# Storing two weight gradients as 4 KB rows in a one-token attention and GEGLU backward kernel

## The chip, the cores and the metric

The kernel runs on one core of a Trainium2 chip. Its time is the device time of one execution in microseconds; six executions of the kernel before gave a median of 285.23 us (284.24 to 286.37). The profile is of one more execution of the same kernel, with every instruction and every DMA packet recorded. The core has a matrix engine (PE, with PEld for its weight loads), a vector engine (DVE), a scalar engine (ACT), a general engine (POOL), a queue for issuing DMAs (SyncE, SP) and 16 DMA engines.

## The reference

A layer adds two branches to its input: attention of one token over a cached window, and a GEGLU feed-forward net. The kernel returns the layer's output and the gradients of all its inputs and weights, for a given gradient `dy` of the output.

```python
xn = layernorm(x)                                  # x: 4 x 1 x 512
q  = (xn @ wq) -> 4 x 32 heads x 128               # wq: 512 x 4096
k, v = last 1024 of 4096 cached rows, 8 kv heads, each used by rep = 4 q heads
p  = softmax(q k^T / sqrt(128));  o = p v          # 4 x 32 x 128
A  = o.reshape(4, 4096) @ wo                       # wo: 4096 x 512
Bf = (gelu(xn @ w_gate) * (xn @ w_up)) @ w_down    # 512 x 1792, 512 x 1792, 1792 x 512
out = x + A + Bf
# returned: out, and d/dx, d/dk_cache, d/dv_cache, d/dwq, d/dwo, d/dw_gate, d/dw_up, d/dw_down of <out, dy>
```

Everything is bf16, sums are fp32. The gradients of the caches are 32 MB each, three quarters of them zeros (the rows outside the window). Two outputs matter here: `out_5`, the gradient of `wo`, which is `o^T dy` over the four batch rows (4096 x 512), and `out_8`, the gradient of `w_down`, which is `a^T dy` with `a` the GEGLU activation (1792 x 512). Each has rows of 512 bf16 values, 1 KB.

## The kernel before, in words

**Stages.** The kernel first loads the three feed-forward weights, does the feed-forward branch forward and backward (to line 687, some 60 us), and then loops over `t` = 0 to 3, each with two kv heads and their eight q heads. In an iteration `kv_steps` transposes the K blocks and makes the scores, `softmax` runs as a chain of small steps, `kv_steps` does the same with V for the gradient of the probabilities, `odq(t, 0)` makes `o` and `odq(t, 1)` makes `dq`, `pre(t + 1)` prepares the next iteration's `q` and `do`, and `fin` adds to the output.

**Background pieces.** The weight and cache gradients are made by small pieces of one or two matmuls, one eviction and, at the last of a group, a store. They stand in one queue, `bg`, and `tick(n)` takes the next n of them in between the foreground steps. The queue is filled with the w_down pieces (`piece_d`), the w_gate and w_up pieces (`piece_g`), and then in every iteration with those of dv, dk, wo (`piece_o`) and wq (`piece_q`). Whatever is left after the loop is run at its end.

**Row form of o and a.** `odq` leaves `o` of one kv head in a tile `od_r` whose 16 used partitions are (batch, head): for a head i of the four, only the four partitions of that head may count in `o^T dy`. Before, this is done on dy's side: `dym` holds four copies of dy, spread over the partitions and masked so that copy i is zero outside the partitions of head i (`spread_rows`, with the mask `msk_i`). `piece_o(g, i)` multiplies `od_r` with copy i into a 128 x 512 block: the 128 rows of head i. For `w_down`, `f_rows` makes the same form `a_r` from the activation: the 16 used partitions are (batch, chunk), and `piece_d(f4, i)` gives the 128 rows of chunk i of a group of four.

**Stores.** An eviction (`evac`, lines 97 and 98) goes to ACT or DVE, whichever has less planned work. The four blocks of a group lie side by side in a tile `osb`, [128, 4, 512], and are stored by one DMA on SyncE's queue. Partition p of the tile holds row p of each of the four blocks, which are 128 rows apart in the output, so the DMA writes 512 rows of 1 KB. The pool of these tiles has four buffers. Stores of zeros from one zero tile (`zero`, 1.5 MB each in rows of 12 KB, 32 in all) are put into the same queue at fixed places, and what is left of them after the loop.

**Order of work around the change.** The order on every engine is the program's. `f_rows` for the activation comes before the loops that transpose w_gate and w_up, which hold 28 slots for pieces. `spread_rows(dy4, dym)` stands between the first feed-forward matmuls and the evictions that follow. `odq(t, 0)` is followed by loads of V for t + 2 and by `pre(t + 1)`; the latter's products `domr` and `qmr` (line 324) are on POOL, and POOL also issues the loads of wo and wq for later iterations (lines 123 and 125).

Of the kernel before, what the change touches and what calls it, by code (L numbers as in the profile page):

```python
# [14 lines left out]
P = 128  # L15
# [3 lines left out]
def kernel(  # L19
# [211 lines left out]
    xnm = const.tile([P, rep, D], BF16, name="xnm")  # L231
    dym = const.tile([P, rep, D], BF16, name="dym")

    def spread_rows(src, dst):
        ps = ps_w.tile([P, D], FP32, name="row_ps", tag="w")
        nc.tensor.matmul(ps[:], lhsT=sel[:], rhs=src[:], start=True, stop=True)
        for i in range(rep):
            if i % 2:
                nc.scalar.activation(out=dst[:, i, :], in_=ps[:], func=ACT.Copy, scale=msk_i[:, i:i + 1])
            else:  # L240
                nc.vector.tensor_scalar(out=dst[:, i, :], in0=ps[:], scalar1=msk_i[:, i:i + 1], scalar2=None,
                                        op0=ALU.mult)
# [196 lines left out]
    def odq(t, k):  # L439
# [11 lines left out]
        else:  # L451
            nc.scalar.activation(out=rows[:], in_=od_ps[:, k], func=ACT.Copy, scale=scale)
        st[t][("o", "dq")[k]] = rows

    def odT(t, k):
# [30 lines left out]
    def dw(t):  # L486
        o_r, dq_r = st[t]["o"], st[t]["dq"]

        def piece_o(g, i, held):
            if i == 0:  # L490
                held["osb"] = outp.tile([P, rep, D], BF16, name="osb_o", tag="o")
            mps = ps_w.tile([P, D], FP32, name="dwo_ps", tag="w")
            nc.tensor.matmul(mps[:], lhsT=o_r[:, g, :], rhs=dym[:, i, :], start=True, stop=True)  # L493
            evac(held["osb"][:, i, :], mps[:], 512)
            if i == rep - 1:
                r0 = (t * HG + g * rep) * Dh
                store(nc.sync, out_5[r0:r0 + rep * Dh, :].rearrange("(h p) n -> p h n", p=P), held["osb"][:], "rest")

# [40 lines left out]
    for wi, wsb in enumerate((wg_sb, wu_sb)):  # L539
        for fc in range(NF):  # L540
            for c in range(ND):
                nc.tensor.matmul(hg_ps[:, wi, fc, :], lhsT=wsb[:, c, fc * P:(fc + 1) * P], rhs=xnT[:, c, :],
                                 start=(c == 0), stop=(c == ND - 1))
    spread_rows(dy4, dym)
    hgu = ffn.tile([P, 2, 4 * NF4, B], FP32, name="hgu")
# [68 lines left out]

    def f_rows(srcT, nm):

        ps = ps_w.tile([P, NF4, P], FP32, name="fr_ps", tag="w")
        for f4 in range(NF4):
            nc.tensor.matmul(ps[0:4 * B, f4, :], lhsT=srcT[:, f4].rearrange("p b i -> p (b i)"),
                             rhs=ident[:], start=True, stop=True)  # L620
        rows = const.tile([P, NF4, P], BF16, name=nm)
        nc.gpsimd.memset(rows[:], 0.0)
        evac(rows[0:4 * B], ps[0:4 * B], 512)
        return rows

    acc_sum(0, [(lambda c, fc=fc: wd_sb[:, fc, c * P:(c + 1) * P], aT_b[:, fc // 4, :, fc % 4]) for fc in range(NF)])
    a_r = f_rows(aT_b, "a_r")

    def piece_d(f4, i, n, held):
        if i == 0:  # L630
            held["osb"] = outp.tile([P, 4, D], BF16, name="osb_d", tag="o")
        mps = ps_w.tile([P, D], FP32, name="dwd_ps", tag="w")
        nc.tensor.matmul(mps[:], lhsT=a_r[:, f4, :], rhs=dym[:, i, :], start=True, stop=True)
        evac(held["osb"][:, i, :], mps[:], 512)
        if i == n - 1:
            store(nc.sync, out_8[4 * f4 * P:(4 * f4 + n) * P, :].rearrange("(h p) n -> p h n", p=P),
                  held["osb"][:, 0:n, :], "rest")
            zero(f4 == 1)
# [13 lines left out]
    for f4 in range(NF4):  # L652
        held = {}
        n = min(4, NF - 4 * f4)
        for i in range(n):
            bg.append(lambda f4=f4, i=i, n=n, held=held: piece_d(f4, i, n, held))
# [133 lines left out]
```

## Time and profile before

| What | Before |
|---|---|
| median of six executions | 285.23 us (284.24 to 286.37) |
| the profiled execution's own time, and its span | 285.14 us, 283.4 us |
| busy: PE, PEld, DVE, ACT, POOL | 202.0, 138.7, 161.1, 117.2, 29.7 us |
| DMA: bytes, packets, mean rate | 112.12 MB, 23,981, 396 GB/s |
| read from HBM, written to HBM | 30.68 MB, 81.01 MB |
| stores osb_o: count, size, median from issue to landing | 8, 512 KB, 18.7 us |
| stores osb_d | 3 of 512 KB, 1 of 256 KB, 7.5 us |
| evictions osb_o: ACT, DVE | 24 of 585 ns, 8 of 690 ns |

The busy times of engines overlap. A span runs from the first to the last instruction, and an execution's time is a little longer than it. In the profile's lines a group is named by its line in the kernel, its engine, its operation and its tiles (`out<-in`); what follows the bar is the busy time, the mean of one in ns, and the idle time in front of it with what ended it. A DMA is "issued" by a queue (SPq, POOLq, ACTq) and "lands" when all its engines have told its semaphore so. The DMA digits and shares are of 16 engines.

### The profile page before, as it was taken

What the parts mean: (1) busy time and instruction counts of PE and PEld (TensorE: products, weight loads), DVE (VectorE), ACT (ScalarE), POOL (GpSimd) and SP (SyncE); (2) the same over time, 40 slices, a digit from 0 to 9 for tenths busy, and PEclk for the clock granted to TensorE, in tenths of its full rate; (3) what the DMA queues carried; (4) which work ended last, traced back from release to release, by engine and by line L of the source; (5) the groups of instructions that cost most, each with busy time, mean ns of one, the idle gap of its engine ahead of it and who ended that gap; (6) DMA issues with size and microseconds to landing.
All of it is one profiled execution on the core that took longest, in us unless ns stands there. A gap on an engine that the chain in (4) does not pass through costs nothing.

```text
span 283.4 us, 6838 instructions
## 1 busy us (share of the span) xinstructions
PE 202.0 (71%) x2963; PEld 138.7 (49%) x2970; DVE 161.1 (57%) x310; ACT 117.2 (41%) x219; POOL 29.7 (10%) x32
## 2 busy tenths in 40 slices
PE   0455998798787889999989998999987974400000
PEld 0444676665556764567665576755556721200000
DVE  7756556476845364678566868567862774810000
ACT  2041484561144438754456645556640664400000
POOL 8400000043000420000610000500000000000000
PEclk9999599799996899999999999999995997955555
DMA  7999999999999999999999999999998999999990
GB/s 268 390 356 421 425 405 409 429 412 339 382 425 406 403 420 416 413 418 418 406 418 413 413 425 418 404 424 425 419 405 359 419 419 420 411 401 396 432 418 26
DMA packets 23981, 112.12 MB, mean 396 GB/s; under 512 B 1664, under 2 KB 10384, under 8 KB 15504
## 3 DMA queue, kind: packets, MB, share of 16 engines
q1 hardware_dynamic: 22160, 103.56, 90.2%
q0 software_dynamic: 1632, 6.29, 5.7%
q10 hardware_dynamic: 160, 1.84, 1.8%
q8 instruction: 23, 0.38, 0.5%
q14 instruction: 6, 0.05, 0.0%
HBM read 30.68 MB, written 81.01 MB: 394 GB/s over the span
## 4 chain that ended last, share of the span: by engine, by line
PE 38%; issue 19%; DMA 11%; DVE 11%; POOL 5%; ACT 3%; POOLq 0%; ACTq 0%; DVEq 0%
PE kv_ps L472 8%; DMA wq_sb<-in_A_wq_dram 7%; PE T_ps L274 7%; PE od_ps L445 5%; PE S_ps L340 5%; DMA out_dram<-stg_dv 4%; PE dwq_ps L506 2%; PE acc_ps L251 2%; DVE wqT L98 2%; PE pT_ps L274 2%; DVE dS_s L362 2%; POOL ztile L167 2%; PE dwo_ps L493 2%; PE woT_ps L274 2%; DVE T_sb L98 2%
## 5 line engine op out<-in xcount | busy, mean ns | idle before, releaser
L98 DVE COPY T_sb<-T_ps 128x1024 bf16<-128x1024 bf16 x64 | 44.1, 689 | 23.5 <-PE T_ps L274 23.4
L97 ACT CAST stg_dv<-kv_ps 128x512 bf16<-128x512 f32 x52 | 28.7, 589 | 29.1 <-PE kv_ps L472 28.4
L97 ACT CAST stg_dk<-kv_ps 128x512 bf16<-128x512 f32 x51 | 28.4, 589 | 24.4 <-PE kv_ps L472 11.0
L472 PE MATMUL kv_ps<-qmr,dS_s 128*128 128x512 bf16 x64 | 22.7, 396 | 5.9 <-ACT stg_dk L97 4.9
L324 POOL TENSOR_TENSOR domr<-r,msk 128x1024 bf16<-128x1024 bf16 x4 | 7.6, 1890 | 149.6 <-DVE r L321 120.1
L472 PE MATMUL kv_ps<-domr,P_s 128*128 128x512 bf16 x60 | 21.2, 399 | 0.2
L274 PE MATMUL T_ps<-ident,vb 128*128 128x128 bf16 x256 | 19.4, 219 | 0.3 <-DVE T_sb L98 0.3
L274 PE MATMUL T_ps<-ident,kb 128*128 128x128 bf16 x256 | 19.5, 219 | 0.2 <-issue 0.2
L274 PEld LDWEIGHTS <-kb 128*128 128x128 bf16 x256 | 16.5, 98 | 4.3 <-issue 0.9
L274 PEld LDWEIGHTS <-vb 128*128 128x128 bf16 x256 | 16.3, 98 | 4.5 <-issue 2.2
L97 ACT CAST osb_q<-dwq_ps 128x512 bf16<-128x512 f32 x26 | 15.0, 586 | 7.3 <-PE dwq_ps L506 6.1
L97 ACT CAST osb_g<-dwg_ps 128x512 bf16<-128x512 f32 (+1 forms) x26 | 12.8, 538 | 10.0 <-PE dwg_ps L645 5.0
L97 ACT CAST osb_o<-dwo_ps 128x512 bf16<-128x512 f32 x24 | 13.8, 585 | 4.3 <-PE dwo_ps L493 3.5
L98 DVE COPY wgT<-wgT_ps 128x1024 bf16<-128x1024 bf16 x14 | 9.6, 689 | 7.9 <-PE wgT_ps L274 7.8
L98 DVE COPY woT<-woT_ps 128x1024 bf16<-128x1024 bf16 x16 | 11.0, 688 | 4.3 <-PE woT_ps L274 3.9
L98 DVE CAST stg_dv<-kv_ps 128x512 bf16<-128x512 f32 x12 | 8.2, 687 | 8.6 <-PE kv_ps L472 8.4
L340 PE MATMUL S_ps<-T_sb,qm 128*32 128x256 bf16 x128 | 12.7, 386 | 0.5 <-DVE T_sb L98 0.5
L340 PE MATMUL S_ps<-T_sb,dom 128*32 128x256 bf16 x128 | 12.7, 387 | 0.0
L98 DVE CAST stg_dk<-kv_ps 128x512 bf16<-128x512 f32 x13 | 8.7, 689 | 6.8 <-DMA out_dram<-stg_dv 5.0
L472 PEld LDWEIGHTS <-dS_s 128*128 128x128 bf16 x64 | 6.1, 98 | 12.6 <-issue 11.5
L493 PE MATMUL dwo_ps<-dym,od_r 128*128 128x512 bf16 x31 | 11.8, 414 | 0.2
L98 DVE COPY wqT<-wqT_ps 128x1024 bf16<-128x1024 bf16 x16 | 10.6, 686 | 2.2 <-PE wqT_ps L274 2.1
(186 smaller groups left out, 372.6 us busy)
## 6 DMA issues: line engine op xcount, KB each, us to landing
out_dram<-ztile SPq DMA_DIRECT2D x32, 1536.0 KB, 18.9
kb<-in_A_k_cache_dram SPq DMA_DIRECT2D x8, 1024.0 KB, 13.1
vb<-in_A_v_cache_dram SPq DMA_DIRECT2D x8, 1024.0 KB, 16.8
out_dram<-stg_dv SPq DMA_DIRECT2D x8, 1024.0 KB, 16.8
out_dram<-stg_dk SPq DMA_DIRECT2D x8, 1024.0 KB, 18.5
out_dram<-osb_o SPq DMA_DIRECT2D x8, 512.0 KB, 18.7
out_dram<-osb_q SPq DMA_DIRECT2D x8, 512.0 KB, 13.3
out_dram<-osb_g SPq DMA_DIRECT2D x8, 448.0 KB, 8.4
```

Source lines behind the costliest of these rows:

```text
L97: return nc.scalar.copy(out=out, in_=in_)
L98: return nc.vector.tensor_copy(out=out, in_=in_)
L167: nc.gpsimd.memset(ztile[:], 0.0)
L251: nc.tensor.matmul(ps[:, c, :], lhsT=lf(c), rhs=rhs, start=(k == 0), stop=(k == len(terms) - 1))
L274: nc.tensor.transpose(ps[:, i, :], a, ident[:])
L324: nc.gpsimd.tensor_tensor(out=mr[:].rearrange("p g q d -> p (g q) d"), in0=r4[:, k, :].unsqueeze(1).broadcast_to([P, SL, Dh]), in1=msk[:]. ...
L340: nc.tensor.matmul(ps[b * RB:(b + 1) * RB, :], lhsT=zt[:, b * GP + g, c0:c0 + RB], rhs=T_sb[:].rearrange("p (x b) -> p b x", b=B)[:, b, :] ...
L362: nc.vector.scalar_tensor_tensor(out=out[:], in0=src[:].unsqueeze(2).broadcast_to([P, WQ, B]), scalar=rr[:, 0:1], in1=mskb[:].unsqueeze(1) ...
L445: nc.tensor.matmul(od_ps[g * 32:g * 32 + B * rep, k, g, :], lhsT=cols[:, jj, g * NQ + q, :], rhs=blks[(t, g)][:, j, :], start=(j == 0), st ...
L472: nc.tensor.matmul(mps[:].rearrange("p q d -> p (q d)"), lhsT=src[:, j * P:(j + 1) * P], rhs=mr[:, g].rearrange("p q d -> p (q d)"), start ...
L493: nc.tensor.matmul(mps[:], lhsT=o_r[:, g, :], rhs=dym[:, i, :], start=True, stop=True)
L506: nc.tensor.matmul(mps[:, i].rearrange("p g d -> p (g d)"), lhsT=xnm[:, i2 * 2 + i, c * P:(c + 1) * P], rhs=dq_r[:].rearrange("p g d -> p ...
```

## The change

The four rows that a partition of `osb` holds become four neighbouring rows of the output instead of four rows that are 128 apart. A partition then writes 4 KB in one piece.

For this, block i of a group must hold the output rows 4 p + i. The weights of its matmul are therefore every fourth column, beginning at i, of a row form that holds all four heads (or chunks) side by side, each nonzero only on its own partitions. So the mask moves from dy to `o` and `a`: `o_s` is `od_r` times the mask `msk_r` for each of the four heads, made by two products on POOL right after `od_r`; `a_s` is made from PSUM by four masked evictions of 16 rows, two on DVE and two on ACT, in place of one eviction to `a_r`. The matmul's other operand is `dyr`, dy spread over the partitions without mask, one eviction in place of the four of `dym`. The last group of w_down has two chunks of 128 rows: it becomes four blocks of 64 rows in place of two of 128, and its store has 64 partitions of 4 KB.

```diff
-    dym = const.tile([P, rep, D], BF16, name="dym")
-
-    def spread_rows(src, dst):
+    dyr = const.tile([P, D], BF16, name="dyr")
+    msk_r = const.tile([P, rep], BF16, name="msk_r")
+    nc.vector.tensor_copy(out=msk_r[:], in_=msk_i[:])
+
+    def spread_rows(src, dst, masked=True):
         ps = ps_w.tile([P, D], FP32, name="row_ps", tag="w")
         nc.tensor.matmul(ps[:], lhsT=sel[:], rhs=src[:], start=True, stop=True)
+        if not masked:
+            evac(dst[:], ps[:], 512)
+            return
         for i in range(rep):
...
         st[t][("o", "dq")[k]] = rows
+        if k == 0:
+            o_s = attw.tile([P, GP, rep, Dh], BF16, name="o_s", tag="o_s", bufs=2)
+            for g in range(GP):
+                nc.gpsimd.tensor_tensor(out=o_s[:, g], in0=rows[:, g].unsqueeze(1).broadcast_to([P, rep, Dh]),
+                                        in1=msk_r[:].unsqueeze(2).broadcast_to([P, rep, Dh]), op=ALU.mult)
+            st[t]["os"] = o_s
...
             mps = ps_w.tile([P, D], FP32, name="dwo_ps", tag="w")
-            nc.tensor.matmul(mps[:], lhsT=o_r[:, g, :], rhs=dym[:, i, :], start=True, stop=True)
+            nc.tensor.matmul(mps[:], lhsT=o_s[:, g].rearrange("p r d -> p (r d)")[:, i:rep * Dh:rep], rhs=dyr[:],
+                             start=True, stop=True)
             evac(held["osb"][:, i, :], mps[:], 512)
             if i == rep - 1:
                 r0 = (t * HG + g * rep) * Dh
-                store(nc.sync, out_5[r0:r0 + rep * Dh, :].rearrange("(h p) n -> p h n", p=P), held["osb"][:], "rest")
+                store(nc.sync, out_5[r0:r0 + rep * Dh, :].rearrange("(p i) n -> p (i n)", i=rep),
+                      held["osb"][:].rearrange("p i n -> p (i n)"), "rest")
...
-    spread_rows(dy4, dym)
+    spread_rows(dy4, dyr, masked=False)
...
-    def f_rows(srcT, nm):
+    def f_rows(srcT, nm, spread=False):
...
+        if spread:
+            rows = ffn.tile([P, NF4, 4, P], BF16, name=nm)
+            nc.gpsimd.memset(rows[:], 0.0)
+            for i in range(4):
+                if i % 2:
+                    nc.scalar.activation(out=rows[0:4 * B, :, i, :], in_=ps[0:4 * B], func=ACT.Copy,
+                                         scale=msk_i[0:4 * B, i:i + 1])
+                else:
+                    nc.vector.tensor_scalar(out=rows[0:4 * B, :, i, :], in0=ps[0:4 * B],
+                                            scalar1=msk_i[0:4 * B, i:i + 1], scalar2=None, op0=ALU.mult)
+            return rows
...
-    a_r = f_rows(aT_b, "a_r")
+    a_s = f_rows(aT_b, "a_s", spread=True)
...
+        m = n * P // 4
         mps = ps_w.tile([P, D], FP32, name="dwd_ps", tag="w")
-        nc.tensor.matmul(mps[:], lhsT=a_r[:, f4, :], rhs=dym[:, i, :], start=True, stop=True)
-        evac(held["osb"][:, i, :], mps[:], 512)
-        if i == n - 1:
-            store(nc.sync, out_8[4 * f4 * P:(4 * f4 + n) * P, :].rearrange("(h p) n -> p h n", p=P),
-                  held["osb"][:, 0:n, :], "rest")
+        nc.tensor.matmul(mps[0:m], lhsT=a_s[:, f4].rearrange("p i f -> p (i f)")[:, i:n * P:4], rhs=dyr[:],
+                         start=True, stop=True)
+        evac(held["osb"][0:m, i, :], mps[0:m], 512)
+        if i == 3:
+            store(nc.sync, out_8[4 * f4 * P:(4 * f4 + n) * P, :].rearrange("(p i) n -> p (i n)", i=4),
+                  held["osb"][0:m].rearrange("p i n -> p (i n)"), "rest")
             zero(f4 == 1)
...
-        for i in range(n):
+        for i in range(4):
             bg.append(lambda f4=f4, i=i, n=n, held=held: piece_d(f4, i, n, held))
```

More of the change, by code (lines that the diff above doesn't have):

```diff
@@ L486, in dw @@
     def dw(t):
-        o_r, dq_r = st[t]["o"], st[t]["dq"]
+        o_s, dq_r = st[t]["os"], st[t]["dq"]
         def piece_o(g, i, held):
```

## The prediction

> **What bounds the kernel now.** I read the occupancy of the page first, because no compute engine fills the span (PE 71%), and then the DMA lines under it.
>
> ```profile
> span 283.4 us, 6838 instructions
> ...
> DMA  7999999999999999999999999999998999999990
> GB/s 268 390 356 421 425 405 409 429 412 339 382 425 406 403 420 416 413 418 418 406 418 413 413 425 418 404 424 425 419 405 359 419 419 420 411 401 396 432 418 26
> DMA packets 23981, 112.12 MB, mean 396 GB/s; under 512 B 1664, under 2 KB 10384, under 8 KB 15504
> q1 hardware_dynamic: 22160, 103.56, 90.2%
> q0 software_dynamic: 1632, 6.29, 5.7%
> ```
>
> The reader is to see a DMA digit of 9 in nearly every slice, and queue shares that add up to 98% with the two small queues. The last compute instruction ends at 249.24 us (dx_b, by the timeline); from there to 283.4 only stores drain. So a microsecond of DMA work is worth up to a microsecond of the end, and compute is worth nothing until it starves the DMA engines. Next I asked for stretches, to see what each row length costs and who ends last (columns: stretch, length, busy PE, PEld, DVE, ACT, POOL, PE clock, DMA share, GB/s).
>
> ```profile
> 12.00:18.00 6.00, 3.06 (x94) 2.53 (x91) 3.31 (x10) 1.30 (x2) 0.00 (x0) 1.00 1.10 354
> 24.00:30.00 6.00, 2.52 (x64) 1.94 (x61) 4.27 (x13) 1.37 (x2) 0.00 (x0) 0.93 1.01 416
> 52.00:58.00 6.00, 5.61 (x91) 4.70 (x92) 3.03 (x6) 2.98 (x7) 0.00 (x0) 0.72 1.02 425
> ...
> 212.00:216.00 4.00, 1.91 (x24) 1.65 (x26) 2.26 (x5) 0.00 (x0) 0.00 (x0) 0.68 0.82 320
> ...
> 264.00:274.00 10.00, 0.00 (x0) 0.00 (x0) 0.00 (x0) 0.00 (x0) 0.00 (x0) 0.50 1.01 426
> 274.00:276.00 2.00, 0.00 (x0) 0.00 (x0) 0.00 (x0) 0.00 (x0) 0.00 (x0) 0.50 1.00 424
> 276.00:278.00 2.00, 0.00 (x0) 0.00 (x0) 0.00 (x0) 0.00 (x0) 0.00 (x0) 0.50 0.26 111
> 278.00:282.40 4.40, 0.00 (x0) 0.00 (x0) 0.00 (x0) 0.00 (x0) 0.00 (x0) 0.50 0.05 22
> ```
>
> 12 to 18 us moves 1 KB rows of weights (354 GB/s), 24 to 30 us 8 KB rows of K and V (416), 52 to 58 us 3.5 KB rows of osb_g among 12 KB rows of zeros (425), 264 to 274 us zeros alone (426). The last two rows matter most: a share of 0.05 is less than one of 16 engines. **One DMA engine ends last**: of the last zero store's semaphore steps in the trace, fourteen come at 276.8 to 276.9 us, one at 278.4, one at 282.4. That engine is late from 23 us on (2.5 us behind the median) and 7 us behind from 180 to 250 us, so what it has to move sets the end; a hole in the other engines' work costs nothing, unless it is longer than that lead.
>
> ```profile
> SPq L785 <- DMA out_dram<-ztile: 19.3, 5, 4.8
> ```
>
> This wait of SyncE shows the same: after the last issue it sits through five zero stores, which land 3.6 to 3.7 us apart.
>
> **The change part by part.** The sum is made against the profiled execution, 285.14 us (span 283.4 and 1.7 around it), 0.1 below the median 285.23.
>
> *Rows.* osb_o (8 x 512 KB) and osb_d (3 x 512, 1 x 256 KB) go from 5,888 rows of 1 KB to 1,472 of 4 KB; bytes, issues and their order stay. On the engine that ends last, the step from the previous store's landing to an osb_o's is 1.14 to 1.55 us, mean 1.34; to an osb_d's 1.29, 1.35, 1.38, and 0.68 for the half one (4.70 together). Rows on both sides of 4 KB: an osb_g takes 1.10 us for 448 KB (1.26 per 512 KB), a K or V load 2.49 us per MB in 8 KB rows (1.24 per 512 KB). I take 1.25 for 512 KB in 4 KB rows: 8 x 0.09 + (4.70 - 3.5 x 1.25 = 0.33) = **1.05, say 1.1 us less**. Bounds: no gain, if the steps' scatter of 0.4 us hides that stores don't pay for short rows; at most the price of 1 KB weight rows, 6.03 MB at 354 instead of 425 GB/s, 17.0 - 14.2 = 2.8 us. In between lie the packets' own durations, by size in the trace: 46 ns for 1 KB, 159 for 4 KB (q0), so 4 x 46 - 159 = 25 ns for 92 rows per engine, 2.3 us; but shares of 1.10 with 1 KB packets say that these durations overlap, so I take the landing steps.
>
> The Trainium skill, "DMA: Bandwidth & Descriptors", section Specifications, says that 512 B are enough for line rate; by it 1 KB rows lose nothing, the change gives 0 and the time stays at 285.2. The 354 GB/s above speak against it. The same page's section "Why small descriptors are slow" has some 3 cycles of overhead per packet of 32-byte beats: an estimate from it is 4 x 35 = 140 cycles against 131 per 4 KB, 6.4% of 14.2 us, 0.9 us.
>
> *a_s instead of a_r.* One 16-row eviction (0.57 us) becomes four, alternating DVE and ACT on one tile. The removed dym shows that such a set runs one after the other:
>
> ```profile
> 15.10 0.75 DVE L241 TENSOR_SCALAR dym<-row_ps,msk_i 128x512 bf16<-128x512 f32 x1 [1.73 <-PE row_ps L236]
> 16.60 0.75 DVE L241 TENSOR_SCALAR dym<-row_ps,msk_i 128x512 bf16<-128x512 f32 x1 [0.76 <-ACT dym L239]
> ...
> 15.88 0.69 ACT L239 ACTIVATE dym<-row_ps,msk_i 128x512 bf16<-128x512 f32 x1 [8.71 <-DVE dym L241]
> 17.39 0.69 ACT L239 ACTIVATE dym<-row_ps,msk_i 128x512 bf16<-128x512 f32 x1 [0.82 <-DVE dym L241]
> ...
> 31.29 0.57 ACT L97 CAST a_r<-fr_ps 16x512 bf16<-16x512 f32 x1 [2.30 <-PE fr_ps L619]
> ```
>
> 15.10 to 18.08 is 3.0 us, so a_s is ready at 34.2 instead of 31.9. Behind the first dwd matmul (32.6 us) the whole of PE waits, some 1.65 us, with the wg transposes; on DVE the first wgT copy goes behind two of the four, on ACT dhg_r's eviction. The first osb_d store is issued near 37.9 instead of 36.2 us. Cover: the engine that ends last is busy with zeros until 42.4, and later in this stage evictions wait for landings anyway:
>
> ```profile
> ACT osb_g L97 <- DMA out_dram<-osb_d: 4.8, 2, 2.8
> ```
>
> The second of these waits ends at 50.2 us by a landing, and the stage starts again from there. Cost 0; without that cover each microsecond past about 2 adds one.
>
> *Two more dwd pieces* (4 for the half chunk): 2 x (0.38 PE + 0.585 ACT). Slots for pieces are 28 in the two weight loops, 10 in pre(0), 16 in the first kv_steps: 54, against 46 pieces before and 48 after. The queue still empties there; cost 0.
>
> *o_s on POOL.* Eight products of 128x512; L324 takes 1.89 us for 1024, so 0.95 each, 1.9 us per t. Behind them on POOL are domr and qmr of the next t and the weight loads; POOL idles 120.1 us before domr (waiting for r4), and after the first od_r (83 us) domr starts only at 95.8. Dwo pieces come 20 us after od_r. Cost 0, above 8 us of lateness what is over.
>
> *dym and masks.* Four evictions (2.9 us) become one (0.6 to 0.7) and a cast of msk_r (0.17, the row of msk). PE waits for wd_sb until 19 us there: that is late next; gain 0. The memset of a_s is four times the 0.5 us of a_r's, at 9 us on POOL, whose next work comes at 60.8 us.
>
> *Weights read with a step of four.* 48 loads. Contiguous 128 columns take 98 to 109 ns; 16 columns take 107 to 115 with a step (L445), 112 to 114 without (L619). Nearest row: no cost. At worst, if a step cost 107 ns per 16 columns, 8 x 107 - 98 = 0.76 us each, 6 us per t, on PE.
>
> *SyncE's issues.* Behind osb_o and osb_q an issue of zeros held SyncE up (7.43 us for three, 8.76 for five):
>
> ```profile
> 210.05 7.43 SPq L103 DMA_DIRECT2D out_dram<-ztile  x3
> ...
> 254.09 8.76 SPq L103 DMA_DIRECT2D out_dram<-ztile  x5
> ```
>
> The hole at 212 to 216 us (share 0.82) falls into the first. With a quarter of osb_o's rows it should shrink, but the last engine had work all through it. Gain 0 by that; fewer rows in the queue can't make an issue wait longer.
>
> Sum: 285.14 - 1.1 = 284.0; against the median, 284.1.
>
> **Rivals.** *A: the full packet price.* The engines pay 25 ns per row: -2.3 us, 282.9. For it: the records; against it: landing steps of 41 ns per KB. *B: nothing.* Stores of 1 KB rows are hidden by overlap, or the late engine's other work grows by as much: 285.2, between 284.7 and 285.7. For it: the steps of single osb_o stores reach down to 1.14. *C: compute becomes late (slower).* Strided weight loads at 0.76 us would put 6 us per t on PE, 24 in all. Slack at the end: the last engine starts the five zero stores at 282.4 - 5 x 3.67 = 264, they are issued from 254.1 and need some 2 us, so 8 us; it decides from there: 24 - 8 - 1.1 = 15 us slower at the bound, 3 at half of it (288). Against it: L445. The change does what it says, so that is no rival.
>
> **How the numbers follow.** Mine 0.50 (283.4 to 284.7), A 0.20, B 0.18, C 0.12. 0.5% is 1.43 us, about what a measurement tells from no change. Faster: 0.17 of A and 0.14 of mine (gain above 1.43 with a scatter of 0.4 in the medians) = 0.31; slower 0.12; same 0.57. The range goes from A's 282.9 less 0.3 for scatter to 286.0, past B; it leaves out most of C and A's tail.
>
> **What would show it.** Packets under 2 KB fall by 5,888, those of 4 KB rise by 1,472; osb_o landing steps near 1.25 us; stretches with osb_o at 420 GB/s or more; the hole near 214 us smaller; still one engine alone in the last 4 us. a_s ready near 34 us, PE idle before the first dwd, and the waits for osb_d landings shorter. LDWEIGHTS of o_s near 100 ns. Wrong if those loads go above 400 ns, if the last engine changes its lag, or if stores start after 60 us with empty engines.

## The result, and the profile after

The changed kernel takes 286.4 us (median of 25 runs, 285.04 to 288.47) against 284.73 us (51 runs, 283.97 to 286.53) for the kernel before: a ratio of 1.0053 with an interval of 1.0041 to 1.0065. By the ratio it is slower by 1.5 us, where 1.1 us less was forecast, and it lies above the range of 282.6 to 286.0. The two profiled spans, 283.4 and 284.5 us, differ by 1.1 us in the same direction.

The page after, its span and its DMA lines:

```profile
span 284.5 us, 6856 instructions
...
DMA  7999969899999999999999999999999999999990
GB/s 267 389 376 431 433 287 393 346 408 352 377 423 384 419 412 426 423 424 423 406 399 419 422 426 420 421 424 421 423 416 406 417 389 422 423 411 421 418 437 33
DMA packets 19565, 112.12 MB, mean 394 GB/s; under 512 B 1664, under 2 KB 4496, under 8 KB 11088
q1 hardware_dynamic: 17744, 103.56, 89.2%
```

The rows changed as they should: packets under 2 KB fall by 5,888, and all packets by 4,416. But the sixth slice (35.6 to 42.7 us) has 287 GB/s where it had 405, and the eighth (50 to 57 us) 346 where it had 429. Both lie in the feed-forward stage, and the missing 118 and 83 GB/s over 7.1 us are 1.4 MB, some 3.4 us at 425 GB/s. As the bytes are the same, somewhat more is moved per us in the rest of the span.

The same stretches of both kernels side by side, before first (columns: stretch, length, busy PE, PEld, DVE, ACT, POOL, granted PE clock, DMA share, GB/s):

```profile
34.00:36.00 2.00, 2.00 (x22) 1.45 (x21) 0.69 (x1) 1.31 (x3) 0.00 (x0) 0.52 1.00 422
36.00:38.00 2.00, 2.00 (x37) 1.52 (x35) 1.31 (x2) 1.69 (x4) 0.00 (x0) 1.00 1.04 442
38.00:40.00 2.00, 2.00 (x37) 1.52 (x35) 1.22 (x3) 1.99 (x5) 0.00 (x0) 1.00 0.93 367
40.00:42.00 2.00, 2.00 (x32) 1.54 (x31) 0.92 (x2) 1.90 (x4) 0.00 (x0) 1.00 1.04 378
```

and after:

```profile
32.00:34.00 2.00, 1.15 (x10) 0.77 (x8) 1.25 (x3) 0.77 (x2) 0.00 (x0) 0.50 1.01 430
34.00:36.00 2.00, 1.27 (x7) 0.76 (x8) 0.47 (x1) 1.69 (x4) 0.00 (x0) 0.50 1.02 436
36.00:38.00 2.00, 2.00 (x21) 1.45 (x20) 0.69 (x1) 1.30 (x3) 0.00 (x0) 0.50 1.00 424
38.00:40.00 2.00, 2.00 (x21) 1.45 (x20) 0.69 (x1) 1.24 (x3) 0.00 (x0) 0.50 0.80 328
40.00:42.00 2.00, 2.00 (x33) 1.50 (x31) 0.95 (x2) 1.35 (x4) 0.00 (x0) 0.84 0.41 162
42.00:44.00 2.00, 2.00 (x32) 1.49 (x29) 1.20 (x3) 1.98 (x4) 0.00 (x0) 1.00 0.63 246
```

From 36 to 40 us PE is full in both, but after the change it gets through 21 matmuls in 2 us instead of 37, because its granted clock is 0.50 instead of 1.00. The records of the clock give the whole stretch: 0.5 from 29.1 to 35.9 us before, from 27.0 to 40.6 us after. From 38 to 44 us the DMA engines have too little to move: shares of 0.80, 0.41, 0.63.

What stands ahead of it is in the timeline after (columns: start, time, engine, line, operation, tiles, idle time before and what ended it):

```profile
31.65 0.74 DVE L644 TENSOR_SCALAR a_s<-fr_ps,msk_i 16x512 bf16<-16x512 f32 x1 [0.31 <-PE fr_ps L633]
...
32.42 0.68 ACT L641 ACTIVATE a_s<-fr_ps,msk_i 16x512 bf16<-16x512 f32 x1 [3.09 <-DVE a_s L644]
33.13 0.74 DVE L644 TENSOR_SCALAR a_s<-fr_ps,msk_i 16x512 bf16<-16x512 f32 x1 [0.75 <-ACT a_s L641]
...
33.91 0.68 ACT L641 ACTIVATE a_s<-fr_ps,msk_i 16x512 bf16<-16x512 f32 x1 [0.81 <-DVE a_s L644]
...
34.73 1.02 PE L660 MATMUL dwd_ps<-dyr,a_s 128*128 128x512 bf16 x2 [1.58 <-ACT a_s L641]
```

Four evictions run one behind the other on two engines, and PE waits 1.58 us for the last: its first dwd matmul starts at 34.73 us. PE's timeline before has no wait there:

```profile
29.03 1.64 PE L251 MATMUL acc_ps<-aT_b,wd_sb 128*128 128x4 bf16 x56 [3.05 <-DVE t L598]
...
32.60 1.06 PE L633 MATMUL dwd_ps<-dym,a_r 128*128 128x512 bf16 x2
```

The stores that follow, by SyncE's timeline, before:

```profile
36.23 2.85 SPq L103 DMA_DIRECT2D out_dram<-osb_d  x2
39.13 1.07 SPq L103 DMA_DIRECT2D out_dram<-ztile  x1
40.85 1.76 SPq L103 DMA_DIRECT2D out_dram<-osb_d  x2
45.68 0.35 SPq L103 DMA_DIRECT2D out_dram<-osb_g  x1
```

and after:

```profile
38.32 4.00 SPq L103 DMA_DIRECT2D out_dram<-osb_d  x2
42.37 0.55 SPq L103 DMA_DIRECT2D out_dram<-ztile  x1
44.14 3.79 SPq L103 DMA_DIRECT2D out_dram<-osb_d  x2
50.22 0.33 SPq L103 DMA_DIRECT2D out_dram<-osb_g  x1
```

By their single issues the four osb_d stores come 2.1, 3.3, 3.3 and 5.5 us later than before, the store of zeros between them 3.2, and the first osb_g 4.5 us. The wait that was to restart the stage, ACT's for a landing of osb_d (4.8 us before), is gone. ACT now waits for PE there:

```profile
DVE wgT L98 <- PE wgT_ps L279: 8.2, 10, 2.2
ACT osb_g L97 <- PE dwg_ps L673: 4.6, 8, 1.6
ACT a_s L641 <- DVE a_s L644: 3.9, 2, 3.1
ACT osb_d L97 <- PE dwd_ps L660: 3.1, 6, 0.7
...
PE dwd_ps L660 <- ACT a_s L641: 1.6, 1, 1.6
```

A ledger makes this a time. On the DMA engine that ends last, the step from the previous store's landing to this one's is what a store takes, plus any time in which the engine had nothing. For the four osb_d and the first three osb_g these steps are 1.29, 1.35, 1.38, 0.68, 1.09, 1.12, 1.09 before, together 8.00 us, and 1.25, 2.60, 1.88, 0.64, 1.51, 1.14, 1.56 after, together 10.58 us. The first osb_d costs no more than before. From the second on the engine has idled, 2.6 us in all against before, and still ends last (by 5.3 us over the median; 5.5 before). The steps of osb_o fall from a mean of 1.34 to 1.29 us, 0.4 us for eight. The ledger is that of one profiled execution, and it leaves out every other store.

**Theory and rivals for the experiments.** Mine, after this reading: the rows gain what was forecast, and the loss is a_s being late, with the half clock that PE's wait prolongs and the two further pieces behind it. Rivals: the further pieces alone; the 64-partition store or the strided weights; the attention half (POOL's products, weights with a step).

### The profile page after: what moved, and what is told of

It reads as the page before. It is cut to its first block, busy times and chain, and to the rows that moved or that the text cites. A ratio compares the mean times of both kernels' runs of the same rounds, so it can differ in the third digit from the quotient of the medians.

```text
span 284.5 us, 6856 instructions
## 1 busy us (share of the span) xinstructions
PE 202.4 (71%) x2962; PEld 138.9 (49%) x2972; DVE 163.8 (58%) x313; ACT 117.9 (41%) x219; POOL 40.1 (14%) x40
## 4 chain that ended last, share of the span: by engine, by line
PE 49%; DMA 17%; DVE 16%; ACT 4%; issue 2%; SPq 0%; DVEq 0%; ACTq 0%
DMA out_dram<-stg_dv 11%; PE T_ps L279 8%; PE kv_ps L484 6%; DMA wd_sb<-in_B_w_down_dram 6%; PE S_ps L345 5%; PE od_ps L450 5%; DVE T_sb L98 3%; PE wgT_ps L279 2%; PE woT_ps L279 2%; DVE dS_s L367 2%; PE dwq_ps L520 2%; PE dwg_ps L673 2%; PE dwd_ps L660 2%; PE acc_ps L256 2%; PE wdT_ps L279 2%
## 5 line engine op out<-in xcount | busy, mean ns | idle before, releaser
L97 ACT CAST stg_dk<-kv_ps 128x512 bf16<-128x512 f32 x52 | 29.2, 588 | 26.2 <-PE kv_ps L484 11.5
L97 ACT CAST stg_dv<-kv_ps 128x512 bf16<-128x512 f32 x51 | 28.1, 588 | 26.3 <-PE kv_ps L484 25.9
L463 POOL TENSOR_TENSOR o_s<-od_r,msk_r 128x512 bf16<-128x512 bf16 x8 | 9.1, 1157 | 106.6 <-DVE od_r L455 77.2
L279 PE MATMUL T_ps<-ident,vb 128*128 128x128 bf16 x256 | 20.9, 229 | 0.6 <-DVE T_sb L98 0.4
L484 PE MATMUL kv_ps<-domr,P_s 128*128 128x512 bf16 x58 | 20.2, 391 | 0.1
L279 PEld LDWEIGHTS <-vb 128*128 128x128 bf16 x256 | 17.7, 103 | 5.3 <-issue 3.7
L505 PE MATMUL dwo_ps<-dyr,o_s 128*128 128x512 bf16 x32 | 12.6, 420 | 0.3 <-ACT stg_dk L97 0.2
L98 DVE CAST stg_dk<-kv_ps 128x512 bf16<-128x512 f32 x12 | 8.0, 687 | 7.8 <-DMA out_dram<-stg_dv 7.0
L520 PE MATMUL dwq_ps<-od_r,xnm 128*128 128x256 bf16 x64 | 11.8, 276 | 0.1
```

The lines of the kernel that those rows point to most:

```text
L97: return nc.scalar.copy(out=out, in_=in_)
L98: return nc.vector.tensor_copy(out=out, in_=in_)
L279: nc.tensor.transpose(ps[:, i, :], a, ident[:])
L463: nc.gpsimd.tensor_tensor(out=o_s[:, g], in0=rows[:, g].unsqueeze(1).broadcast_to([P, rep, Dh]), in1=msk_r[:].unsqueeze(2).broadcast_to([P ...
L484: nc.tensor.matmul(mps[:].rearrange("p q d -> p (q d)"), lhsT=src[:, j * P:(j + 1) * P], rhs=mr[:, g].rearrange("p q d -> p (q d)"), start ...
L505: nc.tensor.matmul(mps[:], lhsT=o_s[:, g].rearrange("p r d -> p (r d)")[:, i:rep * Dh:rep], rhs=dyr[:], start=True, stop=True)
```

## The experiments

The kernels e1 to e4, e5 to e8 and e9 to e12 ran on three chips, each beside the kernel before, which came to 284.60 to 284.69 us there; between these groups the ratios are compared. The table has, for each, the ratio with its interval, the issue times of the first and fourth osb_d and of the first osb_g, and the ledger's sum for the four osb_d and three osb_g on the engine that ends last.

| Kernel | median us | ratio to before | osb_d 1, osb_d 4, osb_g 1 issued | ledger |
|---|---|---|---|---|
| before | 284.73 | 1 | 36.2, 41.9, 45.7 | 8.00 |
| changed | 286.4 | 1.0053 [1.0041, 1.0065] | 38.3, 47.4, 50.2 | 10.58 |
| e1 attention half | 283.64 | 0.9967 [0.9953, 0.9980] | 36.3, 42.4, 45.4 | 8.12 |
| e2 feed-forward half | 287.36 | 1.0095 [1.0074, 1.0116] | 39.5, 47.5, 50.3 | 10.55 |
| e3 1 KB rows | 285.27 | 1.0023 [1.0007, 1.0039] | 36.9, 43.3, 47.4 | 8.82 |
| e4 PE kept busy | 284.13 | 0.9976 [0.9957, 0.9994] | 37.3, 44.8, 47.7 | 9.05 |
| e5 attention half, 1 KB rows | 284.24 | 0.9982 [0.9968, 0.9996] | 35.8, 41.5, 44.5 | 8.08 |
| e6 two pieces fewer | 284.66 | 0.9998 [0.9982, 1.0014] | 38.2, 45.0, 47.9 | 10.07 |
| e7 a_s on POOL, memset behind | 286.67 | 1.0080 [1.0050, 1.0109] | 39.1, 48.5, 50.6 | 10.22 |
| e8 the same, two pieces fewer | 286.23 | 1.0056 [1.0036, 1.0077] | 40.6, 47.9, 50.9 | 10.87 |
| e9 a_s on POOL, memset ahead | 283.47 | 0.9962 [0.9947, 0.9977] | 35.9, 43.6, 45.7 | 7.64 |
| e10 the same, two pieces fewer | 283.69 | 0.9976 [0.9963, 0.9990] | 36.1, 42.0, 45.0 | 7.69 |
| e11 PE kept busy, two pieces fewer | 283.78 | 0.9970 [0.9957, 0.9983] | 37.5, 43.0, 45.8 | 7.83 |
| e12 e10 with PE busy earlier | 283.57 | 0.9961 [0.9948, 0.9974] | 35.5, 41.1, 44.2 | 7.67 |

**e1, the attention half alone.** o_s, dyr and 4 KB rows for out_5; for w_down the masked dym (now for that part alone), a_r and the stores of before.

```diff
+    dyr = const.tile([P, D], BF16, name="dyr")
+    dym = ffn.tile([P, rep, D], BF16, name="dym")
...
     spread_rows(dy4, dym)
+    spread_rows(dy4, dyr, masked=False)
```

> The attention half alone: o_s and 4 KB rows for out_5; the feed-forward half stays as before (a_r, dym, 14 dwd pieces, 1 KB rows). Theory (the loss is made in the feed-forward stage, by a_s that comes late, a PE clock that stays at 0.5 for longer behind the wait, and two more pieces): 0.3 to 0.9 us faster than the kernel before, ratio 0.997 to 0.999; first osb_d store issued near 36.2 us. Rival A (the products on POOL and the strided weight loads cost the time): slower than before by 1 us or more, ratio above 1.003. Rival B (4 KB rows of out_5 are themselves slower to store): landing steps of osb_o above 1.37 us and a ratio above 1.002.

It gains 0.95 us (by the ratio), just above what was expected and short of the packet price of 1.6 us. The eight products on POOL and the weights with a step of four delay nothing that sets the end.

**e2, the feed-forward half alone.** a_s, 16 pieces and 4 KB rows for out_8; dwo as before, from od_r and dym.

```diff
+    a_s = f_rows(aT_b, "a_s", spread=True)
...
-            nc.tensor.matmul(mps[:], lhsT=o_s[:, g].rearrange("p r d -> p (r d)")[:, i:rep * Dh:rep], rhs=dyr[:],
+            nc.tensor.matmul(mps[:], lhsT=o_r[:, g, :], rhs=dym[:, i, :], start=True, stop=True)
```

> The feed-forward half alone: a_s, dyr, 16 dwd pieces and 4 KB rows for out_8; the attention half stays as before (od_r times dym, 1 KB rows). Both dym and dyr are made. Theory: the whole loss and none of the gain of out_5, 1.5 to 2.6 us slower than before, ratio 1.005 to 1.009; first osb_d store near 38.3 us. Rival A: no slower than before, 0.999 to 1.001. Rival B: at most 0.5 us slower, for out_8 alone.

It loses 2.7 us, a little more than expected. The two halves account for the change: 0.9967 times 1.0095 is 1.0062, inside the changed kernel's interval. So the loss is in the feed-forward half, and the attention half's rival falls.

**e3, the whole change with 1 KB rows.** Every block is one head or chunk again, stored as rows of 1 KB; o_s, a_s and 16 pieces stay.

```diff
-        nc.tensor.matmul(mps[0:m], lhsT=a_s[:, f4].rearrange("p i f -> p (i f)")[:, i:n * P:4], rhs=dyr[:],
+        nc.tensor.matmul(mps[:], lhsT=a_s[:, f4, i, :], rhs=dyr[:], start=True, stop=True)
...
-            store(nc.sync, out_8[4 * f4 * P:(4 * f4 + n) * P, :].rearrange("(p i) n -> p (i n)", i=4),
+            store(nc.sync, out_8[4 * f4 * P:(4 * f4 + n) * P, :].rearrange("(h p) n -> p h n", p=P),
```

> The changed kernel with every matmul taking one head's or chunk's 128 neighbouring columns of o_s and a_s, so that blocks and stores are those of before: 1 KB rows; weight loads without a step; everything else as changed. In the short group of w_down the last two of four pieces make zero blocks that are not stored. Theory: rows of 4 KB are worth what the landing steps say, so this is 0.4 to 1.2 us slower than the changed kernel, ratio to before 1.006 to 1.010. Rival B (4 KB rows are the loss): faster than the changed kernel, ratio at or below 1.002. Packet price (25 ns per row and engine): 2.3 us slower than the changed kernel, ratio 1.013.

It was to be slower than the changed kernel and is faster, 1.0023. It doesn't isolate the rows, for it moves the stage too: a slice `a_s[:, f4, i, :]` depends on its own eviction alone, so that the first dwd matmul starts at 32.16 us and not at 34.73. Every fourth column over all four chunks needs all four evictions. So the full wait comes with the step of the weights.

**e4, PE kept busy.** The changed kernel with 16 more transposes, into a tile that nothing reads, just ahead of the first dwd matmul.

```diff
+            if dfq is None:
+                dm_ps = ps_w.tile([P, 2 * ND, P], BF16, name="dm_ps", tag="w")
+                for _ in range(2):
+                    for x in range(2 * ND):
+                        nc.tensor.transpose(dm_ps[:, x, :], wsb[:, x % ND, 0:P], ident[:])
             tick(1)
```

> The changed kernel with 16 more transposes in front of the first dwd matmul, into a tile that nobody reads, so that PE has work while a_s is made. Theory with the clock: the granted clock is back at 1.0 by 37 us instead of 40.6, the second osb_d store is issued near 40.5 us instead of 42.0, and the time is 0.5 to 1.2 us below the changed kernel, ratio to before 1.001 to 1.004. Theory without the clock (the lateness of a_s and the two pieces alone): the stores come as in the changed kernel or later, ratio 1.005 to 1.007.

Adding work takes away 2.2 us, more than expected. The place of PE's wait in its timeline, and the stretches of this kernel, to be read beside those of the changed one above:

```profile
33.01 1.72 PE L711 MATMUL dm_ps<-ident,wg_sb 128*128 128x128 bf16 x16
34.80 0.59 PE L660 MATMUL dwd_ps<-dyr,a_s 128*128 128x512 bf16 x2
```

```profile
32.00:34.00 2.00, 2.00 (x21) 1.82 (x19) 1.25 (x3) 0.70 (x2) 0.00 (x0) 0.50 1.04 442
34.00:36.00 2.00, 1.94 (x25) 1.46 (x24) 0.66 (x2) 1.91 (x4) 0.00 (x0) 0.90 0.99 418
36.00:38.00 2.00, 2.00 (x37) 1.59 (x35) 1.26 (x2) 2.00 (x5) 0.00 (x0) 1.00 1.04 442
38.00:40.00 2.00, 2.00 (x37) 1.56 (x35) 1.38 (x2) 1.97 (x5) 0.00 (x0) 1.00 0.89 360
40.00:42.00 2.00, 2.00 (x32) 1.41 (x29) 1.35 (x2) 1.82 (x4) 0.00 (x0) 1.00 1.00 399
```

a_s is as late as in the changed kernel and the first dwd matmul starts at 34.80 us. But the clock is back at 34.4, not 40.6 us, the second osb_d is issued at 39.4 instead of 42.0, and the DMA engines stay fed. So the start, 2 us late, is nearly covered by itself; the half clock that PE's wait prolongs is not.

**e5, the attention half with 1 KB rows.** As e1, but for the row length of out_5 and the step of the weights.

```diff
-            nc.tensor.matmul(mps[:], lhsT=o_s[:, g].rearrange("p r d -> p (r d)")[:, i:rep * Dh:rep], rhs=dyr[:],
+            nc.tensor.matmul(mps[:], lhsT=o_s[:, g, i, :], rhs=dyr[:], start=True, stop=True)
```

> The attention half alone (o_s on POOL, dyr), but with the blocks of the kernel before: the weights are 128 neighbouring columns of o_s (one head) and osb_o is stored as rows of 1 KB. Beside the attention half it differs in the row length of out_5 and the step of the weights alone. Landing steps: the attention half gains 8 x 0.06 to 0.09, so this kernel should lose it again: 0.4 to 0.95 us slower than the attention half, ratio to before 0.998 to 1.001. If the packets' own durations are the price (25 ns for 64 rows per engine and 1.6 us in all), 1.002 or more. If the attention half's gain came from elsewhere (one eviction in place of four masked ones, no step in the weights), it stays at 0.996 to 0.997.

It is 0.6 us slower than e1 by the medians (0.4 by the ratios), as the landing steps say: osb_o's mean on the engine that ends last is 1.40 us here and 1.31 in e1, 8 x 0.09 = 0.7 us; over all engines 1.36 and 1.29, 0.6 us. But the intervals of e1 and e5 overlap, and e5 is itself 0.4 to 0.5 us faster than the kernel before, with the same rows. What gives that part of the half's gain was not found.

**e6, two pieces fewer.** The changed kernel, but the short group of w_down stays two blocks of 128 rows of 1 KB: 14 dwd pieces.

```diff
+        if n < 4:
+            mps = ps_w.tile([P, D], FP32, name="dwd_ps", tag="w")
+            nc.tensor.matmul(mps[:], lhsT=a_s[:, f4, i, :], rhs=dyr[:], start=True, stop=True)
...
-        for i in range(4):
+        for i in range(4 if n == 4 else n):
```

> The changed kernel, but the short group of w_down stays two blocks of 128 neighbouring columns, stored as 256 rows of 1 KB: 14 dwd pieces instead of 16. a_s is as late and the low clock as long. If the two further pieces matter, the fourth osb_d store comes two loop steps sooner (47.4 becomes 43 to 44) and the first osb_g 2 to 3.5 us sooner (50.2 becomes 47 to 48), and the time falls by 0.5 to 1.5 us: ratio 1.000 to 1.0035. If only the late start and the clock matter, the time stays at 1.005 to 1.0065.

It gives back 1.6 us (by the ratios), and its clock is at 0.5 for 13.7 us as in the changed kernel. So the two pieces do cost, once the stage is late: each takes a place in the queue ahead of osb_g's, and the first osb_g is issued 2.4 us sooner without them. The edit takes away the store of 64 partitions as well, but that store's step was no longer in the changed kernel (0.64 us) than the one of before (0.68).

**e7, a quick a_s, with a mistake.** a_s becomes four tiles, one for each group of chunks: the first made by one DVE product from PSUM, the others by POOL from one ACT eviction `a_q`.

```diff
+            a_q = ffn.tile([P, NF4, P], BF16, name="a_q")
+            evac(a_q[0:4 * B], ps[0:4 * B], 512, eng="act")
+            for f4 in range(NF4):
+                rows = ffn.tile([P, 4, P], BF16, name=f"{nm}{f4}")
+                nc.gpsimd.memset(rows[:], 0.0)
+                eng, src = (nc.vector, ps) if f4 == 0 else (nc.gpsimd, a_q)
+                mk = msk_i if f4 == 0 else msk_r
+                eng.tensor_tensor(out=rows[0:4 * B], in0=src[0:4 * B, f4].unsqueeze(1).broadcast_to([4 * B, 4, P]),
+                                  in1=mk[0:4 * B].unsqueeze(2).broadcast_to([4 * B, 4, P]), op=ALU.mult)
```

> The changed kernel, but a_s is four tiles, one for each group of chunks: the first is one DVE product of the fr_ps bank and the mask, the other three are POOL products from one ACT eviction. All 16 pieces and all 4 KB rows stay. The first dwd matmul should come near 32.7 us, as before the change (34.7 in the changed kernel). If the wait for a_s, with the clock that it keeps low, is the cause of the loss, the clock is back at 1.0 near 36 us, the first osb_d store is issued near 36.5 and the first osb_g near 47 (two more pieces than before), and the time is 283.6 to 284.6: ratio 0.996 to 0.9995. If the loss lies elsewhere, in the 64-partition stores or the strided weights, it stays above 1.004.

The first dwd matmul came at 32.60 us, as before the change, and yet the kernel took 286.67 us. Its timeline shows why:

```profile
35.05 1.03 POOL L645 TENSOR_TENSOR a_s<-a_q,msk_r 16x512 bf16<-16x512 bf16 x1
...
36.03 0.52 POOL L650 MEMSET dhg_r<- 128x512 bf16 x1
...
36.58 0.57 ACT L97 CAST dhg_r<-fr_ps 16x512 bf16<-16x512 f32 x1 [4.82 <-POOL dhg_r L650]
37.06 3.33 ACT L97 CAST osb_d<-dwd_ps 128x512 bf16<-128x512 f32 x6
37.20 0.59 PE L662 MATMUL dwd_ps<-dyr,a_s 128*128 128x512 bf16 x1 [1.09 <-ACT dhg_r L97]
```

On POOL, the memset of the next tile, dhg_r, now stood behind three products. ACT's eviction into dhg_r waited 4.82 us for it, ACT's evictions of osb_d stood behind that one, and PE waited for free PSUM buffers. The clock stayed at 0.5 until 43.0 us. My edit had moved the wait to another queue.

**e8, the same with 14 pieces.** The same mistake, and e6's edit.

> As the kernel with a quick a_s in four tiles, and the short group of w_down as two blocks of 1 KB rows (14 pieces). Nothing in the feed-forward stage should then be later than before the change: first osb_d near 36.3, first osb_g near 45.7. With the attention half's gain (0.95 us) and that of three osb_d stores (3 x 0.07 to 0.1), 283.2 to 283.7: ratio 0.994 to 0.997, at or below the attention half alone. If two more pieces cost nothing once a_s is quick, it equals the former kernel within 0.3 us.

286.23 us, and a clock of 0.5 until 44.5 us (the stage began some 1.5 us later in its profile than in e7's). Its numbers say little of the pieces, but e7 and e8 show the stage late in another way and at a like price: 3.4 us above e9 and 2.3 above e10 by the ratios, where the changed kernel is 2.6 above e9.

**e9, the mistake mended.** All memsets first; the products for the second to fourth group come behind the memset of dhg_r.

```diff
         s_r = f_rows(srcT, nm)
+        if nm == "dhg_r":
+            for f4 in range(1, NF4):
+                spread_a(f4)
```

> The quick a_s in four tiles and all 16 pieces, with one step moved: on POOL the memset of dhg_r now stands ahead of the products for a_s (it was behind them, so that ACT's eviction of dhg_r came at 36.58 us instead of 32.4 and all osb_d evictions behind it). First dwd matmul near 32.6, dhg_r near 32.4, clock 1.0 from about 36, first osb_d near 36.5, first osb_g near 47 to 48 (two pieces more than before). If the time follows the lateness of this stage, as in the kernels so far (osb_g at 45.4: 0.997, 47.7: 0.998, 50.2: 1.005, 50.6: 1.008), it is 283.6 to 284.6, ratio 0.996 to 0.9995. If products on POOL or the separate tiles have a price of their own, it stays above 1.003.

283.47 us, 0.9962: with the 16 pieces, the 4 KB rows, the strided weights and the 64-partition store of the change; only the making of a_s differs. Its timeline and stretches:

```profile
31.50 0.68 DVE L647 TENSOR_TENSOR a_s<-fr_ps,msk_i 16x512 bf16<-16x512 f32 x1 [0.91 <-ACT a_q L97]
31.53 0.57 ACT L97 CAST dhg_r<-fr_ps 16x512 bf16<-16x512 f32 x1
31.54 3.02 POOL L647 TENSOR_TENSOR a_s<-a_q,msk_r 16x512 bf16<-16x512 bf16 x3 [20.13 <-ACT a_q L97]
...
32.23 1.04 PE L666 MATMUL dwd_ps<-dyr,a_s 128*128 128x512 bf16 x2
```

```profile
36.00:38.00 2.00, 2.00 (x36) 1.53 (x32) 1.21 (x3) 1.98 (x4) 0.00 (x0) 1.00 1.00 424
38.00:40.00 2.00, 2.00 (x37) 1.54 (x35) 1.29 (x2) 1.97 (x5) 0.00 (x0) 1.00 0.96 389
40.00:42.00 2.00, 2.00 (x24) 1.31 (x23) 1.41 (x3) 1.39 (x3) 0.00 (x0) 1.00 1.06 432
42.00:44.00 2.00, 2.00 (x29) 1.29 (x29) 1.13 (x2) 1.41 (x4) 0.00 (x0) 1.00 1.01 428
```

PE doesn't wait, the clock is back at 35.2 us, and the DMA share stays at 0.96 or more in these stretches. The ledger is 7.64 us: no idling, and osb_d at 1.25, 1.19, 1.23 and 0.66. Against the changed kernel the ledger falls by 2.9 us, and the time by 2.9 (2.6 by the ratios). The rivals of the strided weights and of the 64-partition store fall with this run.

**e10, the same with 14 pieces.**

> The same with the short group as two blocks of 1 KB rows (14 pieces): first osb_g near 45.5 to 46, as before the change; 283.0 to 283.8, ratio 0.993 to 0.997, at or below the attention half alone (0.9967). If two more pieces cost nothing while the stage is on time, it equals the kernel with 16 pieces within 0.3 us.

283.69 us, no better than e9. With the stage on time no cost of the two pieces shows, though the fourth osb_d is issued 1.6 us later with them.

**e11, PE kept busy and 14 pieces.** e4's and e6's edits together.

> The changed kernel with 14 pieces and with the 16 transposes into a tile that nothing reads ahead of the first dwd matmul: a_s is as late as in the changed kernel (first dwd matmul near 34.8), the clock is back near 35 and two pieces are saved. First osb_d near 37.3, first osb_g near 45.5. If clock and pieces are the two parts of the loss and lateness alone is covered, 283.2 to 284.0, ratio 0.994 to 0.998, that is 0.3 to 1 us below either of the two edits alone. If one of them was enough, it equals the kernel with the transposes alone (0.9976) within 0.3 us.

283.78 us, by the ratios 0.2 us below e4 and 0.8 below e6; the intervals of e4 and e11 overlap. The two don't add up: against the changed kernel, by the ratios, e4 is 2.2 us faster, e6 1.6 and e11 2.4. That either alone brings the stage most of the way back under its cover fits this, but was not tested further.

**e12, PE busy earlier.** e10 with 40 transposes that nothing reads, in PE's wait of 3 us for the vector engine from 26 to 29 us.

```diff
     spread_rows(xn_b, xnm)
+    dm_ps = ps_w.tile([P, 2 * ND, P], BF16, name="dm_ps", tag="w")
+    for x in range(40):
+        nc.tensor.transpose(dm_ps[:, x % (2 * ND), :], wd_sb[:, x % NF, 0:P], ident[:])
```

> The kernel with the quick a_s and 14 pieces, with 40 transposes into a tile that nothing reads in PE's wait of 3 us for the vector engine (26 to 29 us): they end before that wait does. If the wait is what lowers the clock, it stays at 1.0 through the stage (no 0.5 stretch of 6.8 us from 29 us), the first osb_d comes near 35 and the first osb_g near 43.5 to 44.5. That is earlier than before the change, where the engines have zeros to move until 42: gain 0 to 0.7 us over the kernel without them, ratio 0.992 to 0.997. If the clock falls in any case, equal times.

The clock still fell, later and for less long (31.4 to 34.8 us), and the first osb_g came 0.8 us sooner than in e10. The times differ by 0.1 us in the medians and 0.4 in the ratios, and the intervals overlap: no gain of coming sooner is shown. The best kernels, e9 and e12, are by the ratios 1.1 us faster than the kernel before, and 2.6 us faster than the changed one.

## Why the prediction was wrong

**The step that failed** is "a_s instead of a_r", in its words "Cost 0; without that cover each microsecond past about 2 adds one". What it said of the start was right: a_s ready at 34.2 us (34.6 measured), PE waiting "some 1.65 us" (1.58), first osb_d "near 37.9" (38.3). And that first store was covered as it said: the engine that ends last was busy with zeros, landed it at 43.0 us, and its step is 1.25 us.

Two things were missing. First, the lateness was carried on as a constant 1.7 us, while it grew from store to store. The wait fell into a stretch with half the clock, in which a loop step takes 1.93 us instead of 1.08, and that stretch lasted until 40.6 us instead of 35.9 (34.4 in e4, where the wait was filled). By the first osb_g the stage was 4.5 us late. The trace of before showed the half clock, 0.50 and 0.52 in the stretches from 30 to 36 us, and a wait put into it was priced as if the rate stayed the same. Second, the cover was one store's. The second osb_d was issued at 41.96 us instead of 38.69, 1.0 us before the engine that ends last had landed the first, and that was too late for it: its step is 2.60 us instead of 1.35. The second cover, ACT's wait for landings (4.8 us before), was no cover either: it is gone from the waits of the changed kernel, where the DMA engines had run dry.

The price in the same sentence came near: 4.5 us of lateness, less about 2, is 2.5 us. The changed kernel lost 2.6 us against e9, and 2.6 in the ledger against before. e4, with the clock given back and its first osb_g 2.0 us late, shows that the first 2 us are covered, up to about half a microsecond. In the other kernels neither account is that exact: against e9 the ledger has 2.4 us more in e6 and 2.6 in e7, where the times are 1.0 and 3.4 us longer by the ratios; the lateness of the first osb_g less 2 us gives 0.2 and 2.9.

**The rows** came out in the sum, and in part by luck. -1.1 us was said; e9, the change without the late a_s, is 1.1 us below before by its ratio (1.2 by the medians). But e5, with osb_o and osb_d in rows of 1 KB, is already 0.4 to 0.5 us below before, about half of what e1 gains, and e9 is only 0.6 us below e5 by the ratios, with intervals that overlap.

The landing steps give the rows more: osb_d's four went from 4.70 to 4.33 us in e9 (4.375 was said). For osb_o, 0.72 us was said, and e5 to e1 gives 0.4 to 0.6 in the time and 0.6 to 0.7 in the steps. Over all 14 profiles, osb_o's mean step over all engines is 1.36 to 1.40 us in the four kernels with 1 KB rows there (before, e2, e3, e5) and 1.25 to 1.31 in the ten with 4 KB rows, some 0.1 us per store. On the engine that ends last the two groups overlap (1.33 to 1.40 and 1.27 to 1.42), so that how much of this reaches the end is not settled. The bound "nothing" isn't excluded by the times, whose intervals overlap; the full packet price of 2.3 us (rival A) is excluded, by e1 and e9. The Trainium skill's rule that 512 B are enough for line rate ("DMA: Bandwidth & Descriptors", Specifications) was weighed there: here osb_o's steps are 5 to 7% longer with 1 KB than with 4 KB rows (1.40 and 1.31 us on the engine that ends last in e5 and e1, 1.36 and 1.29 over all engines). So for these stores the rule is nearly right. The estimate of 0.9 us from that page's overhead per packet (section "Why small descriptors are slow") lies near what the landing steps give (0.4 us for osb_d, 0.4 to 0.8 for osb_o) and above the 0.6 us between e5 and e9.

**Two more dwd pieces**, "cost 0", held in the case it was worked out for (e9 against e10) and not in the one that came (1.6 us, e6 against the changed kernel). "The queue still empties" was about the end of the stage; what counts is what stands in the queue behind the pieces while the engines starve.

**o_s on POOL** (1157 ns each, not 950, at no cost), **the strided weights** (dwo matmuls 420 ns, 414 before), and **dym and the masks** held as costs of nothing: e1 has the three and gains. **SyncE's issues** were to gain nothing, though the hole from 212 to 216 us should shrink. It shrank (a DMA share of 0.97 instead of 0.82), and the issue of three zeros behind osb_q takes 4.41 us instead of 7.43. But from 226 to 230 us a hole of 0.84 has come up, where before had 1.03, and in e1 and e9 it is 0.79; so no gain by it is shown. Rival C, the slower one, had the right kind of place, compute that becomes late, and the wrong cause. Its chance of 0.12 was for the strided weights alone; a late a_s had been given a cost of zero and so no rival of its own. The two groups of the changed kernel that these readings rest on (what follows the bar is the busy time, the mean in ns, and the idle time before):

```profile
L505 PE MATMUL dwo_ps<-dyr,o_s 128*128 128x512 bf16 x32 | 12.6, 420 | 0.3 <-ACT stg_dk L97 0.2
...
L463 POOL TENSOR_TENSOR o_s<-od_r,msk_r 128x512 bf16<-128x512 bf16 x8 | 9.1, 1157 | 106.6 <-DVE od_r L455 77.2 <-DVE cc L433 29.4
```

**What stays open.** Where e5's 0.4 to 0.5 us come from, with the rows of before. Why one DMA engine lags behind the others through the whole span. How much of the half clock's effect goes through each store was not taken apart further than e4 and e6 do it. What makes the hole from 226 to 230 us was not followed.

## What to carry to other kernels

A delay ahead of a chain of stores isn't covered because its first store is: write down the issue of each store at the rate that the engines will then have, and compare each with when the DMA engines run dry. Where the profile shows PE near a half clock, look at what a wait does to the rate behind it: here filling a wait of 1.6 us with work that nobody reads gave back 2.2 us, and splitting the late tile, so that the first consumer needs only its own part, 2.6. When work is moved to another engine to be quicker, look at what it then stands ahead of in that engine's queue: a memset of 0.5 us behind three products cost as much as the delay that the edit removed.

## What the runs showed of the hardware

PE's granted clock is 0.5 or 1.0 in the records of these kernels, and the lengths of the half stretches in this stage are multiples of one length: 3.4 (e12), 6.8 (before, e4, e5, e9, e11), 10.2 (e1, e2, e3, e10), 13.7 (changed, e6) and 17.1 us (e7, e8). Each kernel has one profiled execution, and where its half stretch begins varies (25.7 to 29.1 us, 31.4 in e12). It ends at 34.4 to 36.7 us in the kernels in which PE didn't wait or was given work (before, e1, e4, e5, e9 to e12), at 38.2 in e3, at 39.4 to 40.6 in those with a wait of 1.6 us (changed, e2, e6), at 43.0 and 44.5 in e7 and e8.

One pattern fits all 14 profiles. Counted from its beginning in steps of 3.41 us, the half stretch ends with the first step that begins when the 56 four-column matmuls ahead of the stage are done (29.03 to 30.67 us before; to within 0.1 us in e4) and in which PE doesn't wait for 0.8 us or more (e12 has a wait of 0.37 in it). Before, that step is 32.5 to 35.9 us, and in e4 31.0 to 34.4. In the changed kernel PE's wait from 33.15 to 34.73 us lies across the border of two steps, at 33.8, and the first step without it is 37.2 to 40.6. So the wait of 1.6 us costs a whole step of 3.4 us at half the clock; the rest of the 4.7 us between 35.9 and 40.6 is where the steps happened to lie. The pattern was read from these traces and not tested by a run of its own.

The Trainium skill, "TensorE: Matmul & The Clock Gate", Part 1, has the two states and a free-running window of some 3.4 us, and the lengths agree with it. It asks for about one busy window to get the full clock back. The traces agree if the window of the four-column matmuls doesn't count as a busy one: before, PE has no idle time in its records from 29.03 us on, and the clock came back at 35.9, after the second window.

A product on POOL takes about as long with 16 partitions (1.03 us, e9) as with 128 (1.16 us), for 512 elements in each.

One DMA engine ends 2.7 to 6.9 us behind the median of the others in every one of these profiles, so the end of this kernel is that of one engine.
